# Local attention and a top-2 mixture of experts in one kernel: the routing steps are handed out by their VectorE time, and the array's products come a turn after what they read

## The chip, the cores and the metric

The kernel runs on one core of a Trainium2 chip. The metric is the device time of one execution, in microseconds (us). A core has five engines that run their own instruction streams in program order: TensorE (PE in the profile, "the array"), VectorE (DVE), ScalarE (ACT), GpSimd (POOL) and SyncE (SP, which here only issues DMAs). They wait for each other by semaphores.

## The reference

Attention within chunks of 64 tokens gives 4608 rows of 512 numbers; a noisy gate then sends each row to the two best of 8 experts, and the two results are added by their weights:

```python
scores = scale * np.matmul(q_c, k_c.transpose(0, 1, 2, 4, 3))   # 8 x 8 x 576 x 64, chunks of 64
attn = softmax(scores)
x = np.matmul(attn, v_c)  ->  x: (4608, 512)
logits = x @ w_gate
noise_scale = np.log1p(np.exp(x @ w_noise))
noisy_logits = logits + noise_scale * noise
top2 = np.argpartition(-noisy_logits, 2, axis=1)[:, :2]          # weights: softmax over the two
for e in range(8):
    for k in range(2):
        mask = top2[:, k] == e
        h = np.maximum(x[mask] @ w1[e], 0.0)                     # w1: 8 x 512 x 1024
        out[mask] += top2_w[mask, k, None] * (h @ w2[e])         # w2: 8 x 1024 x 512
```

## The kernel before, in words

**Three stages.** The 4608 tokens are 36 tiles of 128. `attend(it)` (L677) is one turn of the attention stage: it holds the scores of tile `it` (L410), the product with v of tile `it-2` (L437), the transposes of the probabilities of tile `it-1` (L426) and of the finished rows of tile `it-3` (L457). Every fourth turn adds the gate's products (L464), and the turn after that their sum over four parts (L476). VectorE has four instructions in each turn: the maximum `mx` (L414), the subtraction `pr` (L419), the reciprocal `rc` (L445) and the division `xs` (L449). ScalarE has the exponential (L422) and three copies out of PSUM (L442, L428, L458). SyncE loads q, k and v four turns ahead and stores the finished rows to a DRAM buffer `xbuf`. Turns 36 to 40 finish the last tiles, and four of them lie inside the first expert block.

After that come the expert blocks, 24 of them, three per expert. Block i gathers its rows of `xbuf` by a list, transposes them (`x_tile`, L288, then `xh` L295 on ScalarE and `xl` L296 on VectorE), multiplies by w1 (`layer1`, 8 steps f of 12 matmuls, L305) and by w2 (`layer2`, per 128 rows 8 steps f of 3 matmuls, also L305). All products are made of three, from a high and a low part. So each layer 1 step needs `hh` (L323, ScalarE) and `hl` (L324, VectorE) after it, each layer 2 tile `o` (L343, VectorE), and a store (L272, an indirect DMA that GpSimd issues). During layer 1 of block 0 the w2 of expert 0 is split into its parts (`w2h` L137, `w2l` L138).

**Routing.** The lists are made by `route(g)` (L481) for five groups of tiles: 8, 8, 4, 8 and 8. It is a Python generator; each `yield` ends a step, and its instructions go into the streams where the caller asks for the next step. Per group there are: four ScalarE instructions (L494 to L497), the noisy logits (L501 to L509), the two best of eight (L514, L518), their one-hot form (L523 to L529), a rank by nine small products on the array (L535, L537), positions and weights (L540 to L582; for the last group also an order of the experts, L556 to L572). Then each tile of the group is built: `gohp` half on GpSimd (L598) and half on ScalarE (L599, L600), `geq` on VectorE (L602), `grhs` on GpSimd, in the last group on VectorE (L606); and two products place it into one PSUM bank (L590, four matmul records). Last, the bank is added to `acc` (L624), and after groups 1, 3 and 4 the list of block 0, 1 or 2 is written (`finish_lists`, L207 to L211) and its rows are gathered (L240, indirect DMAs on GpSimd).

**What sets the order.** Nothing is scheduled by the compiler: program order is the order of the calls. Before the change `step_route(n)` takes n steps, whatever they cost: 10 in a turn (15 from turn 35), 2 after each quarter of a layer 1 step and 2 after each layer 2 step of blocks 0 and 1. Only the oldest group moves. `IDLE` puts 7 empty steps where another engine's answer is awaited, and a tile's products follow its `grhs` by some steps:

```python
            yield
            yield
            built.append((r, ohp, rhs))
            if len(built) > 2:
                yield
                place(*built.pop(0))
            yield
```

Of the kernel before, what the change touches and what calls it, by code (L numbers as in the profile page):

```python
# [8 lines left out]
FT = mybir.dt.float32  # L9
# [51 lines left out]
def kernel(ctx, tc, qT, kT, vh, wgn, noise, w1, w2, out, caps=CAPS):  # L61
# [417 lines left out]
    IDLE = 7  # L479

    def route(g):  # L481
# [16 lines left out]
        for _ in range(IDLE):  # L498
            yield

        V.scalar_tensor_tensor(u, u, -1.0, y, op0=OP.add, op1=OP.subtract)  # L501
        yield
        V.tensor_sub(sp, sp, u)
        yield
        V.scalar_tensor_tensor(sp, z[:, :, 1, :], 0.0, sp, op0=OP.max, op1=OP.add)
        yield
        V.tensor_mul(sp, sp, nz[:, t0:t0 + G, :])
        yield
        V.tensor_add(sp, sp, z[:, :, 0, :])  # L509
        yield  # L510
        m = gate.tile(n8, FT, name="gm")
        mi = gate.tile(n8, U32, name="gmi")
        for r in range(G):
            V.max(m[:, r], sp[:, r])  # L514
            if r % 2:
                yield
        for r in range(G):
            V.max_index(mi[:, r], m[:, r], sp[:, r])  # L518
            if r % 2:
                yield  # L520
        oh = gate.tile([P, 2, G, NE], FT, name="goh")
        for k in range(2):
            V.tensor_tensor(oh[:, k], be(e_row), br(mi[:, :, k]), OP.is_equal)  # L523
            yield
# [5 lines left out]
        yield  # L530
        nc.scalar.activation(ex, ex, AF.Exp)
        for _ in range(IDLE + 4 if g == LAST else IDLE):
            yield
        rk = PS[:, 7, 256:256 + 8 * (G + 1)].rearrange("p (g e) -> p g e", e=NE)
# [3 lines left out]
        for _ in range(IDLE):  # L538
            yield
# [4 lines left out]
        yield  # L544
# [3 lines left out]
        yield  # L548
# [3 lines left out]
        yield  # L552
        if g == LAST:
# [10 lines left out]
            yield  # L564
# [8 lines left out]
            yield  # L573
# [3 lines left out]
        yield  # L577
        pj = gate.tile([P, 2, 2, G], I32, name="gpj")
        pf = gate.tile([P, 2, 2, G], FT, name="gpf")
# [3 lines left out]
        yield  # L583

        lp = PS[:, 7, 0:2 * NL]
        built = []

        def place(r, ohp, rhs):
            for k in range(2):
                nc.tensor.matmul(lp, ohp[:, k], rhs[:, k].rearrange("p c n -> p (c n)"),  # L590
                                 start=(r == 0 and k == 0), stop=(r == G - 1 and k == 1))
# [3 lines left out]
        for r in range(G):  # L595
            t = t0 + r
            ohp = gate.tile([P, 2, P], FT, name="gohp", bufs=3)
# [6 lines left out]
            yield  # L604
            rhs = gate.tile([P, 2, 2, NL], FT, name="grhs", bufs=3)
            B.tensor_tensor(rhs, eq[:, :, None, :].to_broadcast([P, 2, 2, NL]),  # L606
                            vals[:, :, t, :, None].to_broadcast([P, 2, 2, NL]), OP.mult)
            yield
            yield
            built.append((r, ohp, rhs))  # L610
            if len(built) > 2:
                yield
                place(*built.pop(0))
            yield
        while built:
            for _ in range(3):
                yield
            place(*built.pop(0))
        yield
# [11 lines left out]
        if g == LAST:  # L631
            for c in range(2):
                for js in (slice(0, NJ // 2), slice(NJ // 2, NJ)):
                    n = [P, js.stop - js.start, NE, NE]
                    by = gate.tile([P, 2, 2, NL], FT, name="grhs", bufs=3).rearrange("p a b n -> p (a b n)")
# [4 lines left out]
                    yield  # L640
# [15 lines left out]
    def finish_route(until=lambda: not routing):  # L656
        while not until():
            step_route(1)
# [18 lines left out]
    def attend(it):  # L677
        STEPS = 2 if it < 35 else 3
# [15 lines left out]
        if it - 5 >= 0 and (it - 5) % 4 == 3:  # L694
            gate_sum((it - 5) // 4)
            if grp_of[it - 5] != grp_of.get(it - 4):
                routing.append(route(grp_of[it - 5]))
# [41 lines left out]
    def hook_tail(f, d):  # L739
# [6 lines left out]
        else:  # L746
            step_route(2)

    for i in range(NBL + 1):
# [27 lines left out]
        def hook2_r(k, f):  # L777
            hook2_f(k, f)
            step_route(2)
# [11 lines left out]
        if i < NBL:  # L791
            layer1(i, hook1, hook_tail if i == 0 else lambda f, d: step_route(2))
# [160 lines left out]
```

## Time and profile before

| | |
|---|---|
| median of 3 runs | 1007.67 us (1004.89 to 1007.74) |
| the profiled execution's own time | 996.2 us |
| its span in the trace | 994.4 us |
| PE, DVE, ACT, POOL busy | 96%, 46%, 31%, 49% of the span |
| VectorE's first `mx` of the attention stage, and its last | 5.4 us and 132.1 us |
| the first expert matmul (L305) | 139.2 us |

The profile gives times in us from the start of the span. A row of the timeline has start, duration, engine, line, operation, out<-in and count; what stands in brackets is how long the engine had been idle before it, and who ended that. A row of the groups has the busy time of the group in us and the mean of one instruction in ns. The share "PEclk" is the array's granted clock, 1.00 being full speed. Busy shares are averages over stages with different limits, so each stage is read by itself.

### The profile page before, as it was taken

To read this page: it belongs to the slowest core of one execution; us is meant where nothing else is said; L and a number is where in the kernel's file an instruction comes from. 1 tells how busy PE (TensorE), PEld (TensorE's weight loads), DVE (VectorE), ACT (ScalarE), POOL (GpSimd) and SP (SyncE) were. 2 spreads that over 40 slices of the span, in tenths; PEclk is the share of its full clock that TensorE was granted. 3 is DMA by queue.
4 is the path that set the end of the run, shared out by engine and by line. 5 is a ranking of instruction groups with operands and counts; after the bars stand their busy time and mean duration, and the time that the engine had idled before them with its cause. 6 is when DMAs were issued, how large, how long until landed. Compare 5 with 4: busy or idle time off the path is not lost.

```text
span 994.4 us, 18553 instructions
## 1 busy us (share of the span) xinstructions
PE 955.1 (96%) x7353; PEld 855.4 (86%) x7353; DVE 459.3 (46%) x1001; ACT 307.9 (31%) x689; POOL 485.4 (49%) x619
## 2 busy tenths in 40 slices
PE   6898989999999999999999999999999999999994
PEld 5677769888799998998899899989998999899984
DVE  6678876543445442534253434343444344434311
ACT  4667764312232221322131223122322231223100
POOL 1043534426677776177617772677167616601111
PEclk9989999999999999999999999999999999999998
DMA  9998968332513452245214522552245223511212
GB/s 336 377 340 271 323 228 310 63 102 54 146 46 81 111 151 50 44 122 150 51 33 128 148 51 36 135 140 58 68 96 140 58 70 94 136 20 22 32 25 41
DMA packets 60362, 121.54 MB, mean 122 GB/s; under 512 B 9280, under 2 KB 10176, under 8 KB 60272
## 3 DMA queue, kind: packets, MB, share of 16 engines
q1 hardware_dynamic: 40112, 81.64, 23.2%
q0 software_dynamic: 20160, 38.69, 20.8%
q8 instruction: 58, 0.95, 0.4%
q14 instruction: 32, 0.26, 0.1%
HBM read 81.56 MB, written 38.73 MB: 121 GB/s over the span
## 4 chain that ended last, share of the span: by engine, by line
PE 84%; DVE 2%; ACT 1%; issue 0%; POOL 0%; DVEq 0%; ACTq 0%; POOLq 0%
PE PS L305 80%; PE PS L590 1%; PE PS L334 1%; PE PS L288 0%; DVE xl L296 0%; ACT xh L295 0%; PE PS L464 0%; DVE o L343 0%; POOL grhs L606 0%; DVE xs L449 0%; PE PS L222 0%; ACT xt L458 0%; PE PS L437 0%; ACT gohp L599 0%; DVE gmi L518 0%
## 5 line engine op out<-in xcount | busy, mean ns | idle before, releaser
L260 POOL DMA_INDIRECT xg<-xbuf,piece x257 | 265.9, 1035 | 72.6 <-issue 66.3
L305 PE MATMUL PS<-xh,w1h 128*128 128x384 f32 (+2 forms) x768 | 262.9, 342 | 1.9 <-ACT xh L295 1.1
L305 PE MATMUL PS<-xl,w1h 128*128 128x384 f32 (+2 forms) x768 | 260.5, 339 | 0.3 <-DVE xl L296 0.3
L305 PE MATMUL PS<-xh,w1l 128*128 128x384 f32 (+2 forms) x768 | 260.6, 339 | 0.0
L272 POOL DMA_INDIRECT out<-o,lid x73 | 116.9, 1601 | 246.5 <-DVE o L343 234.4
L305 PE MATMUL PS<-w2h,hh 128*128 128x512 f32 x584 | 229.5, 393 | 0.0
L305 PE MATMUL PS<-w2h,hl 128*128 128x512 f32 x584 | 228.4, 391 | 0.0
L305 PE MATMUL PS<-w2l,hh 128*128 128x512 f32 x584 | 228.3, 391 | 0.0
L323 ACT ACTIVATE hh<-PS 128x384 fp32r<-128x384 f32 (+1 forms) x192 | 93.9, 490 | 362.3 <-PE PS L305 362.3
L324 DVE SCALAR_TENSOR_TENSOR hl<-PS,hh 128x384 fp32r<-128x384 f32 (+1 forms) x192 | 107.0, 558 | 181.1 <-ACT hh L323 181.1
L343 DVE TENSOR_SCALAR o<-PS,lwt 128x512 f32<-128x512 f32 x73 | 54.7, 749 | 235.4 <-PE PS L305 235.4
L305 PEld LDWEIGHTS PS<-xh,w1h 128*128 128x128 f32 x768 | 144.3, 188 | 5.4 <-ACT xh L295 1.5
L305 PEld LDWEIGHTS PS<-xl,w1h 128*128 128x128 f32 x768 | 144.3, 188 | 2.3 <-DVE xl L296 0.5
L305 PEld LDWEIGHTS PS<-xh,w1l 128*128 128x128 f32 x768 | 144.2, 188 | 0.9
L305 PEld LDWEIGHTS PS<-w2h,hl 128*128 128x128 f32 x584 | 109.5, 188 | 23.6
L305 PEld LDWEIGHTS PS<-w2h,hh 128*128 128x128 f32 x584 | 109.7, 188 | 23.2 <-issue 0.8
L305 PEld LDWEIGHTS PS<-w2l,hh 128*128 128x128 f32 x584 | 109.7, 188 | 22.4
L295 ACT ACTIVATE xh<-y 128x512 fp32r<-128x512 f32 x67 | 41.2, 615 | 104.8 <-DVE y L292 104.8
L598 POOL TENSOR_SCALAR gohp<-row_p,gpf 128x128 f32<-128x128 f32 x36 | 25.1, 707 | 95.8 <-DVE gpf L582 71.6
L296 DVE TENSOR_TENSOR xl<-y,xh 128x512 fp32r<-128x512 f32 x67 | 45.0, 672 | 48.0 <-ACT xh L295 48.0
L292 DVE STREAM_TRANSPOSE y<-xg 128x512 f32<-128x512 f32 x67 | 45.6, 680 | 3.2 <-DMA xg<-xbuf,piece 3.2
L138 DVE TENSOR_TENSOR w2l<-st,w2h 128x512 fp32r<-128x512 f32 x64 | 44.4, 693 | 0.0
(139 smaller groups left out, 783.7 us busy)
## 6 DMA issues: line engine op xcount, KB each, us to landing
st<-in_w SPq DMA_DIRECT2D x56, 512.0 KB, 5.0
out<-zero SPq DMA_DIRECT2D x37, 256.0 KB, 4.0
vb<-in_vh SPq DMA_DIRECT2D x36, 260.0 KB, 4.9
qp<-in_qT SPq DMA_DIRECT2D x36, 256.0 KB, 4.5
kb<-in_kT SPq DMA_DIRECT2D x36, 256.0 KB, 5.3
xbuf<-xs SPq DMA_DIRECT2D x36, 256.0 KB, 4.4
xg<-xbuf,piece POOLq DMA_INDIRECT x257, 2.7
st<-in_w SPq DMA_DIRECT2D x16, 256.0 KB, 5.7
```

The lines of the kernel that those rows point to most:

```text
L138: (eng or nc.vector).tensor_sub(lo[:, s], st[:, s], hi[:, s].bitcast(FT))
L260: nc.gpsimd.indirect_dma_start(out=XG[e, j][:, t * P:(t + 1) * P], out_offset=None, in_=xpieces, in_offset=bass.IndirectOffsetOnAxis(ap=pi ...
L272: s = nc.gpsimd.indirect_dma_start(out=to, out_offset=bass.IndirectOffsetOnAxis(ap=rows, axis=0), in_=o, in_offset=None, compute_op=OP.add)
L292: nc.vector.transpose(y[:, 0:4 * r], x[:, 0:4 * r])
L295: nc.scalar.activation(oh, src, AF.Copy)
L296: nc.vector.tensor_sub(ol, src, oh.bitcast(FT))
L305: nc.tensor.matmul(p, a, b, start=first and n == 0, stop=last and n == 2)
L323: nc.scalar.activation(hh[:, 0:m], p, AF.Relu)
L324: nc.vector.scalar_tensor_tensor(hl[:, 0:m], p, 0.0, hh[:, 0:m].bitcast(FT), op0=OP.max, op1=OP.subtract)
L334: nc.tensor.matmul(p[32 * q:32 * q + 32, 0:P], HF[0][:, f, 32 * t:32 * t + 32], w[:, q * P:(q + 1) * P], start=(f == 0), stop=(f == NF - 1))
L343: nc.vector.tensor_scalar(o[0:r], p[0:r], weights_of(i, j)[0:r], None, op0=OP.mult)
L598: nc.gpsimd.tensor_scalar(ohp[:, 0], row_p, pf[:, 0, 0, r:r + 1], None, op0=OP.is_equal)
```

## The change

Routing steps now yield what they cost on VectorE in us (0.15 to 0.8). `step_route(us, n)` moves a counter `clock` on by n and hands out steps until their sum has used up `us`: 1.3 us and n = 6 in an attention turn, 0.6 and 0.5 after each quarter of a layer 1 step in blocks 0 and 1, 1.0 and n = 2 after each layer 2 step. A `yield None` makes the group wait until the counter has moved on by `TURN` = 6, `yield "next"` until it has moved at all. When the oldest group waits, the next one is given steps, up to the point where it would need the shared PSUM bank. A tile costs `TILE` = 0.6, so up to three tiles are built in a turn (before: two), and a tile's products are placed when it is `TURN` old or when more than two are built. `gohp` and `grhs` get four buffers (before: three), `gpj` and `gpf` two. The rank goes to bank 6 while an older group holds bank 7.

```diff
-    IDLE = 7
+    TURN, TILE = 6, 0.6
+    clock, turn, flushing = [0], [0], []
...
         nc.scalar.activation(sp, u, AF.Ln)
-        for _ in range(IDLE):
-            yield
+        yield None
...
         V.scalar_tensor_tensor(u, u, -1.0, y, op0=OP.add, op1=OP.subtract)
-        yield
+        yield 0.22
...
         nc.scalar.activation(ex, ex, AF.Exp)
-        for _ in range(IDLE + 4 if g == LAST else IDLE):
-            yield
-        rk = PS[:, 7, 256:256 + 8 * (G + 1)].rearrange("p (g e) -> p g e", e=NE)
+        yield None
+        while routing[0][0] != g and (turn[0] % 4 == 2 or turn[0] in (NT - 4, NT - 3) or turn[0] > NT):
+            yield "next"
+        at = 7 if routing[0][0] == g else 6
+        rk = PS[:, at, 256:256 + 8 * (G + 1)].rearrange("p (g e) -> p g e", e=NE)
         nc.tensor.matmul(rk, before, ohb, start=True, stop=False)
...
+        while routing[0][0] != g:
+            yield "next"
...
         for r in range(G):
+            while built and (clock[0] - built[0][3] >= TURN or len(built) > 2):
+                place(*built.pop(0))
             t = t0 + r
-            ohp = gate.tile([P, 2, P], FT, name="gohp", bufs=3)
+            ohp = gate.tile([P, 2, P], FT, name="gohp", bufs=4)
...
-            built.append((r, ohp, rhs))
-            if len(built) > 2:
-                yield
-                place(*built.pop(0))
-            yield
+            built.append((r, ohp, rhs, clock[0]))
+            yield TILE
         while built:
-            for _ in range(3):
-                yield
+            while clock[0] - built[0][3] < TURN and not flushing:
+                yield "next"
             place(*built.pop(0))
...
-    def step_route(n):
-        for _ in range(n):
-            while routing:
+    def step_route(us, n=1):
+        clock[0] += n
+        for item in list(routing):
+            while us > 0:
+                if clock[0] < item[2] and not flushing:
+                    break
                 try:
-                    next(routing[0])
+                    cost = next(item[1])
+                except StopIteration:
+                    routing.remove(item)
                     break
-                except StopIteration:
-                    routing.pop(0)
+                if isinstance(cost, float):
+                    us -= cost
+                else:
+                    item[2] = clock[0] + (1 if cost else TURN)
+            if us <= 0:
+                return
...
-            step_route(5 * STEPS)
+            step_route(1.3, TURN)
...
-            step_route(2)
+            step_route(0.6)
...
-            step_route(2)
+            step_route(1.0, 2)
...
-            layer1(i, hook1, hook_tail if i == 0 else lambda f, d: step_route(2))
+            layer1(i, hook1, hook_tail if i == 0 else lambda f, d: step_route(0.5))
```

The order of the instructions moves at many places; three of them matter below. The lines of `route` lie 1 to 5 higher in the new file (L590, the placing, is L593 there; L598 is L603; L602 and L606 are L607 and L610).

The first place is VectorE in turns 12 and 13, where group 0 starts: four instructions of attention make a turn, and `gu` is the first routing step that reads what ScalarE made. Before:

```order
L414 TENSOR_REDUCE mx<-PS 128x8
L419 TENSOR_TENSOR pr<-PS,mx 128x2x4x64
L445 RECIPROCAL rc<-rc 128x8
L449 TENSOR_TENSOR xs<-PS,rc 128x2x4x64
L501 SCALAR_TENSOR_TENSOR gu<-gu,gy 128x64
L503 TENSOR_TENSOR gsp<-gsp,gu 128x64
L505 SCALAR_TENSOR_TENSOR gsp<-gz_655,gsp 128x64
```

After:

```order
L449 TENSOR_TENSOR xs<-PS,rc 128x2x4x64
L414 TENSOR_REDUCE mx<-PS 128x8
L419 TENSOR_TENSOR pr<-PS,mx 128x2x4x64
L445 RECIPROCAL rc<-rc 128x8
L449 TENSOR_TENSOR xs<-PS,rc 128x2x4x64
L501 SCALAR_TENSOR_TENSOR gu<-gu,gy 128x64
L503 TENSOR_TENSOR gsp<-gsp,gu 128x64
L505 SCALAR_TENSOR_TENSOR gsp<-gz_655,gsp 128x64
L507 TENSOR_TENSOR gsp<-gsp,nz 128x64
```

The first `xs` of the second piece is that of turn 12: `gu` has moved behind the four instructions of turn 13.

The second place is the array in layer 2 of block 0, second tile of rows (steps f = 0 and 1 of it, then f = 2). `w2h`, `w2l` are the parts of w2, `hh`, `hl` those of the hidden rows. Before:

```order
L305 MATMUL PS<-w2h_2984,hh_2825 128x512
L305 MATMUL PS<-w2l_2985,hh_2825 128x512
L305 MATMUL PS<-w2h_2984,hl_2826 128x512
L305 MATMUL PS<-w2h_2984,hh_2827 128x512
L305 MATMUL PS<-w2l_2985,hh_2827 128x512
L305 MATMUL PS<-w2h_2984,hl_2828 128x512
L305 MATMUL PS<-w2h_3069,hh_2829 128x512
```

After:

```order
L305 MATMUL PS<-w2h_2962,hh_2834 128x512
L305 MATMUL PS<-w2l_2963,hh_2834 128x512
L305 MATMUL PS<-w2h_2962,hl_2835 128x512
L305 MATMUL PS<-w2h_2962,hh_2836 128x512
L305 MATMUL PS<-w2l_2963,hh_2836 128x512
L305 MATMUL PS<-w2h_2962,hl_2837 128x512
L593 MATMUL PS<-grhs,gohp 128x160 x2
L305 MATMUL PS<-w2h_3045,hh_2838 128x512
```

The first placing of the last group (L593) now stands after 30 of the 72 layer 2 matmuls of block 0; before, it stood in layer 1 of block 1, after all 72 and 9 more. The rank of that group (L537, L539) now stands after 9 of them, before after 42.

The third place is GpSimd in the same stage, from the gather of block 1's rows (`xg<-xbuf`) on: `out<-o` are the stores of block 0. Before:

```order
L240 DMA xg<-xbuf,lid_124 128x512 x3
L271 MEMSET spacer 1x1
L272 DMA out<-o,lid_123 4736x512
L271 MEMSET spacer 1x1
L272 DMA out<-o,lid_123 4736x512
L598 TENSOR_SCALAR gohp<-row_p,gpf 128x128 x2
L271 MEMSET spacer 1x1
L272 DMA out<-o,lid_123 4736x512
L598 TENSOR_SCALAR gohp<-row_p,gpf 128x128 x6
```

After:

```order
L240 DMA xg<-xbuf,lid_124 128x512 x3
L271 MEMSET spacer 1x1
L272 DMA out<-o,lid_123 4736x512
L603 TENSOR_SCALAR gohp<-row_p,gpf 128x128 x8
L240 DMA xg<-xbuf,lid_125 128x512 x3
```

All eight `gohp` of the last group have moved between the first and the second store. On VectorE the same stage now has, in this order: the rest of the rank's one-hots, the last `hl` and `w2l`, positions and order of the experts, `xl` of block 1's first tile, `o` of block 0's first tile, and then the eight pairs of `geq` and `grhs`; before, three `o`, the third `xl` and two `hl` stood among those.

More of the change, by code (lines that the diff above doesn't have):

```diff
@@ L497, in route @@
         nc.scalar.activation(sp, u, AF.Ln)
-        for _ in range(IDLE):
-            yield
+        yield None
         V.scalar_tensor_tensor(u, u, -1.0, y, op0=OP.add, op1=OP.subtract)
-        yield
+        yield 0.22
         V.tensor_sub(sp, sp, u)
-        yield
+        yield 0.22
         V.scalar_tensor_tensor(sp, z[:, :, 1, :], 0.0, sp, op0=OP.max, op1=OP.add)
-        yield
+        yield 0.22
         V.tensor_mul(sp, sp, nz[:, t0:t0 + G, :])
-        yield
+        yield 0.22
         V.tensor_add(sp, sp, z[:, :, 0, :])
-        yield
+        yield 0.22
         m = gate.tile(n8, FT, name="gm")
@@ L515, in route @@
             if r % 2:
-                yield
+                yield 0.16
         for r in range(G):
@@ L519, in route @@
             if r % 2:
-                yield
+                yield 0.15
         oh = gate.tile([P, 2, G, NE], FT, name="goh")
@@ L537, in route @@
             nc.tensor.matmul(rk[:, k:G + 1], ones, ohb[:, 0:G + 1 - k], start=False, stop=(k == G))
-        for _ in range(IDLE):
-            yield
+        yield None
         V.tensor_scalar(sm, ex, 1.0, 1e-9, op0=OP.add, op1=OP.add)
@@ L547, in route @@
         V.reciprocal(wt[:, 0], sm)
-        yield
+        yield 0.4
         ohr = gate.tile([P, 2, G, NE], FT, name="gohr")
@@ L576, in route @@
         V.tensor_mul(wt[:, 1], ex, wt[:, 0])
-        yield
-        pj = gate.tile([P, 2, 2, G], I32, name="gpj")
-        pf = gate.tile([P, 2, 2, G], FT, name="gpf")
+        yield 0.45
+        pj = gate.tile([P, 2, 2, G], I32, name="gpj", bufs=2)
+        pf = gate.tile([P, 2, 2, G], FT, name="gpf", bufs=2)
         V.tensor_scalar(pj[:, 0], lii[:, :, ts], NE * (P - 1), None, op0=OP.bitwise_and)
@@ L603, in route @@
                             pf[:, 1, :, r:r + 1].to_broadcast(n2), OP.is_equal)
-            yield
-            rhs = gate.tile([P, 2, 2, NL], FT, name="grhs", bufs=3)
+            rhs = gate.tile([P, 2, 2, NL], FT, name="grhs", bufs=4)
             B.tensor_tensor(rhs, eq[:, :, None, :].to_broadcast([P, 2, 2, NL]),
                             vals[:, :, t, :, None].to_broadcast([P, 2, 2, NL]), OP.mult)
-            yield
-            yield
-            built.append((r, ohp, rhs))
-            if len(built) > 2:
-                yield
-                place(*built.pop(0))
-            yield
+            built.append((r, ohp, rhs, clock[0]))
+            yield TILE
         while built:
-            for _ in range(3):
-                yield
+            while clock[0] - built[0][3] < TURN and not flushing:
+                yield "next"
             place(*built.pop(0))
-        yield
+        yield "next"
         av = acc.rearrange("p c n -> p (c n)")
@@ L634, in route @@
                     n = [P, js.stop - js.start, NE, NE]
-                    by = gate.tile([P, 2, 2, NL], FT, name="grhs", bufs=3).rearrange("p a b n -> p (a b n)")
+                    by = gate.tile([P, 2, 2, NL], FT, name="grhs", bufs=4).rearrange("p a b n -> p (a b n)")
                     by = by[:, 0:n[1] * NE * NE].rearrange("p (j r e) -> p j r e", r=NE, e=NE)
@@ L677, in attend @@
     def attend(it):
-        STEPS = 2 if it < 35 else 3
+        turn[0] = it
         if it < NT:
@@ L696, in attend @@
             if grp_of[it - 5] != grp_of.get(it - 4):
-                routing.append(route(grp_of[it - 5]))
+                routing.append([grp_of[it - 5], route(grp_of[it - 5]), 0])
         if it - 4 >= 0 and (it - 4) % 4 == 3:
```

23 lines of the change are left out of this document (12 added, 11 removed).

## The prediction

> **What bounds the kernel now.** The chain of waits is first: the array's instructions are most of it. Next I read busy time by stretches (start:end in us; length; busy time and count of PE, PEld, DVE, ACT, POOL; clock; DMA share; GB/s).
>
> ```profile
> 41.00:112.74 71.74, 62.70 (x1512) 52.72 (x1502) 57.61 (x183) 54.04 (x139) 31.73 (x40) 0.95 0.92 315
> 49.96:56.79 6.83, 6.19 (x100) 5.27 (x91) 6.43 (x38) 3.15 (x7) 0.00 (x0) 0.50 0.98 340
> 165.45:166.78 1.33, 1.33 (x9) 1.24 (x8) 1.18 (x7) 0.69 (x3) 0.00 (x0) 1.00 1.03 380
> 179.84:183.64 3.80, 3.80 (x21) 3.17 (x19) 3.35 (x21) 0.00 (x0) 1.59 (x1) 1.00 0.36 39
> 236.00:990.00 754.00, 745.95 (x4014) 676.68 (x4012) 303.03 (x502) 183.57 (x386) 403.49 (x505) 1.00 0.35 83
> ```
>
> The array ends the chain, and from 236 us on it is busy for 745.95 of 754.00 us. The change touches nothing there, so whatever time the array loses or wins before 236 us moves the end by as much. Two stretches count: the attention stage, and blocks 0 and 1. In the first of them the waits between 41 and 63 us (who waits, for whom; total, times, longest) show what sets the turns:
>
> ```profile
> PE PS L410 <- DVE pr L419: 2.5, 2, 1.8
> DVE gu L501 <- ACT gsp L497: 2.3, 1, 2.3
> ...
> DVE gr L546 <- PE PS L537: 1.6, 1, 1.6
> ```
>
> VectorE stands for 2.3 us because its routing step `gu` follows in the same turn the four ScalarE instructions that it reads. Then the array waits up to 1.8 us for VectorE's `pr`, and in the stretch from 49.96 us, right after it, its clock is 0.50 for 6.83 us. In blocks 0 and 1 (136 to 236 us) these are all the array's waits but one of 1.1 us:
>
> ```profile
> PE PS L305 <- ACT xh L295: 1.1, 1, 1.1
> PE PS L305 <- DVE hl L324: 0.8, 1, 0.8
> PE PS L535 <- DVE gohb L527: 0.6, 1, 0.6
> PE PS L305 <- DVE xl L296: 0.3, 1, 0.3
> ```
>
> So in the blocks there are under 4 us to win, and since the array has no slack there, every placing or rank that comes before its operands costs in full. That is why each of them is timed below: when the array is there, by its matmuls, and when VectorE and GpSimd are, by the instructions ahead.
>
> **Attention: what the turns gain.** With `gu` a turn later its 2.3 us of wait lie beside the next turn's work; the same goes for `gr`, 1.6 us: 3.9 us in all, and the clock's fall goes with the first. Against it stands GpSimd, which now has up to three tiles in a turn (groups of L598, L606 and of the w1 parts, 62 to 110 us; busy, mean ns, idle):
>
> ```profile
> L606 POOL TENSOR_TENSOR grhs<-geq,vals 128x320 f32<-128x320 f32 x16 | 11.6, 723 | 0.8 <-DVE geq L602 0.8
> L598 POOL TENSOR_SCALAR gohp<-row_p,gpf 128x128 f32<-128x128 f32 x16 | 10.7, 669 | 65.6 <-DVE gpf L582 58.9 <-PE PS L437 6.8
> L138 POOL TENSOR_TENSOR w1l<-st,w1h 128x512 fp32r<-128x512 f32 x8 | 10.3, 1282 | 9.2 <-ACT w1h L137 9.2
> ```
>
> Three tiles are 3 × (0.669 + 0.723) = 4.18 us, with a `w1l` 5.46 us, more than the 4.25 us between two `mx` at 112.81 and 117.06 us. Such turns give back some; I take a gain of 3.4 us until turn 31 (ends 1.4 and 5.3: GpSimd giving back 2.5 of the 3.9, or nothing, with 1.4 more from the clock).
>
> **Attention: what the gather takes back.** The list of block 0 and the first gather behind it, and the array's first transposes of those rows:
>
> ```profile
> 112.74 0.17 DVE L211 CAST lid<-lfl 128x3 int32<-128x3 f32 x1
> 112.81 0.69 DVE L414 TENSOR_REDUCE mx<-PS 128x8 f32<-128x512 f32 x1
> ...
> 117.06 0.67 DVE L414 TENSOR_REDUCE mx<-PS 128x8 f32<-128x512 f32 x1
> ```
>
> ```profile
> L240 POOL DMA_INDIRECT xg<-xbuf,lid x1: 1203/1203/1203, 113.2 to 113.2; - x1
> ...
> DMA to landing us min/median/max: 6.6/6.6/6.6
> ```
>
> ```profile
> 124.03 0.60 PE L288 MATMUL PS<-ident,xg 128*128 128x128 f32 x4
> ```
>
> Before, the rows are there at 113.2 + 6.6 = 119.8 us, 4.2 us ahead of the array. After, group 1's bank is added up at the end of turn 31 rather than 29, two turns later. With the 3.4 us that is 112.74 + 2 × 3.8 − 3.4 = 116.9 us (3.8 us is my estimate of these turns, between the 4.25 above and the shorter ones that follow), and the rows land at about 123.8 us. The array comes at 124.03 − 3.4 = 120.6 us, with some 1.3 us of other work that it has before the first transposes; it waits about 1.9 us. Whatever the turns gain moves both alike. Attention's net is −3.4 + 1.9 = **−1.5 us** (ends +0.5 and −3.4).
>
> **Layer 1 of block 0.** The wait for `hl` at 147.17 us follows a placing group that moves away: **−0.8**. Group 3's placings now start after 48 of the 96 matmuls, at the end of step f = 3. From there on, the array's pace (the chain of waits in order of time: start, length, instructions):
>
> ```profile
> 163.24 1.04 PE PS L305 x6
> 164.29 0.54 PE PS L590 x4
> ...
> 171.63 4.81 PE PS L305 x21
> ```
>
> A w1 matmul is 0.173 us, a placing of four records 0.54, a w2 matmul 0.229. A placing every three matmuls comes each 3 × 0.173 + 0.54 = 1.06 us, while GpSimd makes a tile in 1.39 us by the groups above, about 1.3 where the two overlap. The first placing waits behind this chain of step f = 2, whose anchor in before is:
>
> ```profile
> 150.56 0.96 PE L476 MATMUL PS<-sel,ls 128*128 128x16 f32 x8
> ```
>
> ```profile
> 153.32 0.65 DVE L602 TENSOR_TENSOR geq<-row_je,gpf 128x160 f32<-128x160 f32 x2
> ```
>
> The first `geq` came 2.76 us after the sums began; with GpSimd's `grhs`, 0.72, a placing could go at about 3.9 us (0.4 for the semaphores and the `geq` itself), and the array, with 12 matmuls and 0.8 us of sums, is there at 2.9. So it waits 1.0, and then 4 × (1.3 − 1.06), some 0.9, until `gohp` and `grhs` have caught up: **+1.9 us** (ends 0, if both are made while the array still has its step to do, and 4.0).
>
> **The last group's rank** now stands after 9 w2 matmuls. From group 3's last placing the array needs 18 × 0.173 + 9 × 0.229 = 5.2 us. VectorE needs the sum into `acc` and the list (1.33 us, the stretch from 165.45), the steps L501 to L529, and between them the last `hl` and `w2l`:
>
> ```profile
> 168.08 0.22 DVE L501 SCALAR_TENSOR_TENSOR gu<-gu,gy 128x64 f32<-128x64 f32 x1
> ...
> 172.30 0.69 DVE L296 TENSOR_TENSOR xl<-PS,xh 128x512 fp32r<-128x512 f32 x1 [0.94 <-ACT xh L295]
> 172.91 0.21 DVE L523 TENSOR_TENSOR goh<-row,gmi 128x64 f32<-128x64 f32 x1
> ...
> 173.39 0.74 DVE L343 TENSOR_SCALAR o<-PS,lwt 128x512 f32<-128x512 f32 x1
> ```
>
> ```profile
> L324 DVE SCALAR_TENSOR_TENSOR hl<-PS,hh 128x384 fp32r<-128x384 f32 x16 | 8.7, 555 | 13.5 <-ACT hh L323 13.5
> L138 DVE TENSOR_TENSOR w2l<-st,w2h 128x512 fp32r<-128x512 f32 x8 | 5.5, 693 | 0.0
> ```
>
> The steps are (172.30 − 0.94 − 168.08) + (173.39 − 172.91) = 3.76 us. Instructions overlap by some 0.05 to 0.08 us, so `hl` and `w2l` count 0.5 and 0.6. In all 1.33 + 0.1 + 3.76 + 0.5 + 0.6 = 6.3, and the array waits **+1.1 us**.
>
> **The last group's first placing** stands after 30 w2 matmuls. Without waits the array is there at 5.2 + 0.2 (nine small products, an estimate) + 21 × 0.229 = 10.2 us, and with the wait for the rank and the transposes of block 1's first tile (0.6, as in the row of L288) at 11.9. VectorE goes on from 6.3: the last `hl` and `w2l` (with ScalarE's `hh` ahead, which stands behind the exponential that L529 releases) to 8.5; L540 to L582 in 3.80 us (the stretch from 179.84); between them `xl` 0.6 and `o` 0.7: 13.6 us. Then GpSimd:
>
> ```profile
> 174.41 1.65 POOL L272 DMA_INDIRECT out<-o,lid  x1 [3.69 <-DVE o L343]
> 175.47 0.62 POOL L271 MEMSET spacer<- 1x1 f32 x1
> ```
>
> The store of block 0's first tile stands ahead of the eight `gohp`, and GpSimd is free 175.47 − 174.41 = 1.06 us after `o`; the first `gohp` takes 0.67 and its semaphore, 0.8: 15.4 to 15.5 us. The array waits **+3.7 us** (ends 0 and 4.5). Behind it wait the two later tiles of layer 2, and nobody else's work fills the array. The next placings come each 3 × 0.229 + 0.54 = 1.2 us, against 0.67 for GpSimd's part of a tile, so they don't wait.
>
> **The clock.** A wait of 1.8 us was followed by two stretches of 3.4 us at 0.50 in before. In the wait of 3.7 us a stretch of that length is mostly idle, and the array, which is then never idle, does 3.4 us of its work at half speed: 1.7 us lost: **+1.7** (ends 0 and 3.4, two such stretches). [...]
>
> **Start of block 1's layer 1.** The list of block 2 has moved ahead of the third `xl`; the waits for `xh` and `xl` (1.1 + 0.3) become about 1.9: **+0.5** (ends 0 and 1.5). The rest costs nothing: SP's order does not change, no matmul is added, four buffers for three take no time, and the `w1l` of GpSimd move by some tiles in stretches where the array does not wait for them.
>
> **Sum:** −1.5 − 0.8 + 1.9 + 1.1 + 3.7 + 1.7 + 0.5 = +6.6 us. The profiled execution would go from 996.2 to 1002.8 us; it lies 11.5 us under the median, whose runs reach from 1004.89 to 1007.74 us, so I add the sum to the median: 1007.67 + 6.6 = 1014.3 us.
>
> **Rivals.** 0.3%, about what a measurement of this kernel can tell, is 3.0 us.
>
> [...]
>
> *The last group does not hold the array* (0.22): if VectorE's steps overlap more, or ScalarE's `hh` come earlier, so that its `gpf` is done before 10.2 us instead of 13.6, the waits of 1.1 and 3.7 and the clock's 1.7 go: +6.6 − 6.5 = +0.1, 1007.8 us. Against it stands that the lengths are measured and the order is fixed.
>
> *VectorE alone sets the attention turns* (0.16), the faster side. Between 41 and 112.74 us it is busy for 57.61 of 71.74 us (the first stretch) and idles 14.1; if that all goes, because no turn has to wait for what another engine made in it, attention's net is −14.1 + 1.9 = −12.2 instead of −1.5, and the sum is 6.6 − 10.7 = −4.1: 1003.6 us. It decides from a gain of 13 us on (6.5 if the last group does not hold the array). GpSimd's 5.46 us in a turn speak against it.
>
> *A later gather and a second fall of the clock* (0.08): the list 1.9 us later, since GpSimd's tiles lengthen, and another 3.4 us at half speed in layer 1: 6.6 + 1.9 + 1.7 = +10.2, 1017.9 us.
>
> That the change doesn't do what it says is excluded by the order of the instructions, printed above.
>
> **The numbers.** The forecast has 0.40; slower is 0.40 + 0.14 + 0.08 = 0.62, same 0.22, faster 0.16. The range reaches from 1003.5, at the faster case, to 1017.5, just under the last rival; the likeliest case's own range, with attention's and the clock's ends, is 1010.5 to 1017.5.
>
> **What would show it.** Right: `gu` without idle time before it; the array waiting for `xg` at the first transposes of block 0; waits of L593 for `grhs` in layer 1 of block 0 and for `gohp` or `grhs` after 30 w2 matmuls of its layer 2, near 3.7 us, with a stretch at 0.50 behind. Wrong: the first expert matmul over 5 us earlier than 139.2, or no wait at that placing.

## The result, and the profile after

The changed kernel takes 1015.23 us (median of 5 runs, 1014.32 to 1017.39) where the kernel before takes 1004.89 (5 runs, 1003.11 to 1007.74): +10.3 us, ratio 1.010, 95% interval 1.0075 to 1.0125. It is slower, as forecast; the forecast sum was +6.6 us.

The chips differ. Beside eight of the ten experiments below the kernel before takes 996 us, beside the other two 1002.6. The first trace of the kernel before is of 996.2 us, the first trace of the change of 1015.23 us, so the two cannot be subtracted. The changed kernel was therefore traced a second time, where the kernel before takes 996.16 us (experiment after_again, 1006.41 us), and rows below are from that second trace unless the text says otherwise. Two executions took far longer than all others, one of late_last (1916.66 us) and one of the kernel before beside after_again (1591.54 us): the medians count them, the ratios do not.

One piece of the difference between the first two traces can be named. It is the group of products L334 in block 3's stage, of the change and then of the kernel before (busy, mean ns, idle before and its releaser):

```profile
L334 PE MATMUL PS<-st,hf 128*32 128x128 f32 x128 | 7.2, 347 | 2.4 <-issue 2.4
```

```profile
L334 PE MATMUL PS<-st,hf 128*32 128x128 f32 x128 | 3.7, 273 | 0.0
```

The array waits 2.4 us in it for nothing that the profile shows, and its clock is 0.50 from 327.15 to 330.57 us. The second trace of the change has 3.7 us and no wait there, as the kernel before; so the change alone does not make it.

Now the chain of waits of the first trace of the change, by engine:

```profile
PE 79%; issue 2%; DVE 2%; SPq 1%; POOL 1%; DMA 0%; ACT 0%; POOLq 0%; ACTq 0%; DVEq 0%
```

The array still ends it. The array's waits in blocks 0 and 1 (136 to 260 us of the second trace; total, times, longest) answer to the four rows of before:

```profile
PE PS L593 <- POOL gohp L603: 3.8, 1, 3.8
PE PS L305 <- DVE xl L296: 1.8, 1, 1.8
PE PS L537 <- DVE gohb L527: 1.2, 2, 0.9
PE PS L593 <- POOL grhs L610: 1.1, 3, 0.8
PE PS L222 <- DVE xv L218: 1.1, 1, 1.1
```

The wait for `hl` is gone, and 3.85 us for the last group's first `gohp` have come. In the stretches of the second trace behind such waits (the clock is the third number from the end of a row), six have a clock under full speed:

```profile
178.40:181.80 3.40, 1.46 (x5) 1.46 (x6) 2.19 (x6) 0.95 (x4) 3.40 (x5) 0.76 0.61 78
181.80:185.20 3.40, 3.40 (x16) 2.98 (x16) 1.85 (x5) 1.82 (x6) 2.22 (x4) 0.73 0.27 98
198.80:202.20 3.40, 2.93 (x13) 2.93 (x14) 1.08 (x2) 0.15 (x1) 2.88 (x4) 0.78 0.76 169
202.20:205.60 3.40, 3.40 (x16) 3.40 (x15) 0.56 (x1) 0.80 (x2) 0.00 (x0) 0.72 0.79 165
229.40:232.80 3.40, 3.40 (x21) 3.06 (x21) 0.65 (x2) 0.00 (x0) 0.70 (x1) 0.79 0.00 0
232.80:236.20 3.40, 3.40 (x14) 2.63 (x14) 0.96 (x2) 0.60 (x1) 2.00 (x3) 0.71 0.06 19
```

Each pair is one spell of half speed of about 3.4 us: (0.24 + 0.27) × 3.4 = 1.73 us lost, (0.22 + 0.28) × 3.4 = 1.70, (0.21 + 0.29) × 3.4 = 1.70. They lie behind the waits of 3.85, 1.83 and 1.14 us. The kernel before has one, behind its 1.14 us wait for `xv`:

```profile
219.00:222.40 3.40, 3.35 (x19) 3.15 (x20) 0.65 (x2) 0.00 (x0) 0.00 (x0) 0.74 0.00 0
222.40:225.80 3.40, 3.40 (x15) 2.75 (x14) 0.75 (x1) 0.59 (x1) 1.91 (x3) 0.76 0.06 19
```

In the attention stage of the second trace the clock is whole from 41 to 61.26 us, where before had 6.83 us at half:

```profile
41.00:61.26 20.26, 17.28 (x486) 14.45 (x475) 16.80 (x65) 13.87 (x34) 0.00 (x0) 1.00 1.02 371
```

The account of the two stages, before and the change's second trace: the first expert matmul at 139.2 and 139.1 us; from there to block 2's first matmul 91.2 and 101.5 us; the span 994.4 and 1004.8. Between these two traces all 10.3 us lie in blocks 0 and 1. They are made of waits of the array, 3.9 and 9.4 us; of L305, 72.0 and 74.9; of the placings, 7.0 and 8.9 (for each matmul the time until the next one starts, without waits).

The first trace of the change divides its time otherwise: its first expert matmul is at 145.5 us, and from there to block 2 it takes 98.4 us, 7.2 more than before. Its blocks have the same waits (9.4 us) and placings (9.0), but L305 takes 71.8 us, since one spell of half clock lies in them and not three. What its attention stage lost can't be told, since no trace of the kernel before was taken beside it.

### The profile page after: what moved, and what is told of

Its sections match the earlier page's. It is cut to its first block, busy times and chain, and to the rows that moved or that the text cites. A ratio compares the mean times of both kernels' runs of the same rounds, so it can differ in the third digit from the quotient of the medians.

```text
span 1013.3 us, 18557 instructions
## 1 busy us (share of the span) xinstructions
PE 961.6 (95%) x7353; PEld 857.8 (85%) x7353; DVE 462.8 (46%) x1001; ACT 309.6 (31%) x689; POOL 479.6 (47%) x619
## 4 chain that ended last, share of the span: by engine, by line
PE 79%; issue 2%; DVE 2%; SPq 1%; POOL 1%; DMA 0%; ACT 0%; POOLq 0%; ACTq 0%; DVEq 0%
PE PS L305 77%; PE PS L334 1%; SPq L678 1%; PE PS L593 1%; POOL gohp L603 0%; DMA out<-zero 0%; PE PS L288 0%; POOL grhs L610 0%; DVE xl L296 0%; DVE gaccp L638 0%; DVE grhs L636 0%; POOL xg L240 0%; DVE o L343 0%; DVE xs L449 0%; PE PS L222 0%
## 5 line engine op out<-in xcount | busy, mean ns | idle before, releaser
L260 POOL DMA_INDIRECT xg<-xbuf,piece x257 | 260.3, 1013 | 78.7 <-issue 63.3
L305 PE MATMUL PS<-xl,w1h 128*128 128x384 f32 (+2 forms) x768 | 260.4, 339 | 1.8 <-DVE xl L296 1.8
L305 PE MATMUL PS<-xh,w1h 128*128 128x384 f32 (+2 forms) x768 | 261.8, 341 | 0.0
L305 PE MATMUL PS<-xh,w1l 128*128 128x384 f32 (+2 forms) x768 | 260.4, 339 | 0.0
L305 PE MATMUL PS<-w2h,hh 128*128 128x512 f32 x584 | 229.5, 393 | 0.0
L305 PE MATMUL PS<-w2h,hl 128*128 128x512 f32 x584 | 228.1, 391 | 0.0
L305 PE MATMUL PS<-w2l,hh 128*128 128x512 f32 x584 | 228.0, 390 | 0.0
L305 PEld LDWEIGHTS PS<-xl,w1h 128*128 128x128 f32 x768 | 144.2, 188 | 3.9 <-DVE xl L296 2.1
L305 PEld LDWEIGHTS PS<-xh,w1h 128*128 128x128 f32 x768 | 144.3, 188 | 3.1 <-issue 0.8
L305 PEld LDWEIGHTS PS<-xh,w1l 128*128 128x128 f32 x768 | 144.2, 188 | 0.9
L343 DVE TENSOR_SCALAR o<-PS,lwt 128x512 f32<-128x512 f32 x73 | 54.5, 749 | 192.0 <-PE PS L305 142.0
L305 PEld LDWEIGHTS PS<-w2h,hl 128*128 128x128 f32 x584 | 109.4, 187 | 23.5
L305 PEld LDWEIGHTS PS<-w2h,hh 128*128 128x128 f32 x584 | 109.4, 187 | 23.0 <-issue 0.8
L305 PEld LDWEIGHTS PS<-w2l,hh 128*128 128x128 f32 x584 | 109.4, 187 | 22.2
L603 POOL TENSOR_SCALAR gohp<-row_p,gpf 128x128 f32<-128x128 f32 x36 | 26.6, 820 | 93.0 <-DVE gpf L583 92.0
```

The lines of the kernel that those rows point to most:

```text
L260: nc.gpsimd.indirect_dma_start(out=XG[e, j][:, t * P:(t + 1) * P], out_offset=None, in_=xpieces, in_offset=bass.IndirectOffsetOnAxis(ap=pi ...
L305: nc.tensor.matmul(p, a, b, start=first and n == 0, stop=last and n == 2)
L343: nc.vector.tensor_scalar(o[0:r], p[0:r], weights_of(i, j)[0:r], None, op0=OP.mult)
L603: nc.gpsimd.tensor_scalar(ohp[:, 0], row_p, pf[:, 0, 0, r:r + 1], None, op0=OP.is_equal)
```

## The experiments

Theory behind the first four: the change loses in both stages, by its turns of three tiles and late groups in the first, and in the second since the array meets the last group's rank and placings before their operands. Rivals: chance between executions, and that the next late thing takes over when one wait is moved.

**before_again.** No edit.

> The kernel before, unchanged, for a second profiled execution. The two traces differ by 13.5 us at the start of block 2 and by 19.4 us from block 4 on; the extra 5.9 us lie in one run of the array's L334 products (9.8 us instead of 3.9, with gaps in which the array waits for no engine). Theory: those 5.9 us are not the change's; they come and go from one execution to the next, and the first profile of before (994.4 us) was a lucky one. Then this one has such gaps somewhere behind 236 us and a span of 1000 to 1006 us, with the first expert matmul at 139 us and block 2's start near 230 us again. Rival: the gaps are the change's own; then the span is 994 to 997 us again.

Measured: 996.54 us, span 994.7; first expert matmul 139.7, block 2 at 230.9 us, no gap in L334. The rival's number, though not its reason: after_again shows that the gap is not the change's either. It goes with the chip in all twelve traces: the nine from chips where the kernel before takes 996 us have no gap there, the three others have one.

**old_attention.** The counters are those of before until the expert blocks begin (a step per yield, 7 for `yield None`, 10 steps in a turn, the oldest group alone), and a tile's products are placed as before:

```diff
+        if old:
+            for _ in range(10 if turn[0] < 35 else 15):
+                if debt[0]:
+                    debt[0] -= 1
+                    continue
...
     attend(NT)
+    old.clear()
```

> The changed kernel, with the steps of the attention turns (up to turn 36) handed out as before: the array's order up to the first expert matmul is that of before, and from there on that of the change. Theory: the change loses in both stages, 6.3 us up to the first expert matmul and 7.2 us from there to block 2. Then the first expert matmul is at 139 us (138.5 to 140.5) instead of 145.5, the stretch from there to block 2 still takes 98 us, and the time is 5 to 7 us under the changed kernel's: 1009 to 1011 us. Rival: the attention stage is limited by what does not change (DMA, the clock, chance), and the first expert matmul stays at 143 us or later: 1013 to 1016 us.

Measured: 1007.92 us, ratio 1.0109 (1.0092 to 1.0126). Its trace has the first expert matmul at 143.4 us in the very order of the kernel before, and the blocks take 101.6 us. A miss, and for the first expert matmul the rival's number: the attention stage of before, alone, saves nothing against the 1.0102 of after_again. The blocks are as in after_again, three spells included. The time at the 19th maximum was 70.9 us here and 66.6 and 67.1 in the two traces of before, with one order: the first turns vary by some 4 us.

**late_last.**

```diff
         n2 = [P, 2, NL]
+        if g == LAST:
+            yield None
+            yield None
```

> The changed kernel, where the last group waits two TURNs more between its positions and its first tile, so that its first placing stands after 48 of the layer 2 matmuls of block 0 instead of 30. Theory: the wait of 3.85 us at that placing and the half clock behind it (1.7 us) go, since 18 matmuls (4.1 us) have moved in front of it: 5 us less, 1009 to 1011 us, and no wait over 1 us there. Rival: what is late next takes the place of it (the stores, now ahead of the tiles on GpSimd, or the placings that move towards block 1): a wait of 2 us or more elsewhere before block 2, and 1013 to 1016 us.

Measured: 1005.16 us, ratio 1.0091 (1.0068 to 1.0115). The array's longest waits in blocks 0 and 1 of its trace:

```profile
PE PS L305 <- DVE xl L296: 2.7, 1, 2.7
PE PS L593 <- DVE geq L610: 2.2, 1, 2.2
```

The placing's wait fell from 3.85 to 2.2 us, and the one for `xl` rose from 1.8 to 2.7: the first expert matmul to block 2 takes 97.7 us. The rival holds in the main. On VectorE the second `xl`, for which it stands 2.07 us until ScalarE's `xh` is there, and the second `o` now stand between the `geq` of that group, so moving the steps of one group later doesn't free the array. One spell of half clock lies in these blocks, and none behind the 2.7 us.

**fast_chain.**

```diff
-            yield TILE
+            yield 1.0 if turn[0] < NT else TILE
...
-            step_route(1.3, TURN)
+            step_route(2.0, TURN)
```

> The changed kernel with 2.0 us of steps in an attention turn instead of 1.3, and a tile that costs 1.0 there instead of 0.6, so that a group is ready for its tiles a turn or two earlier and two tiles are built in a turn instead of three. Theory: in the attention stage the change loses by turns of three tiles (5.1 us each, GpSimd busy throughout) and by late groups; with two a turn these turns take 4.5 us or less and the first expert matmul comes at 141 to 143 us: 1011 to 1013 us. Rival: the time of these turns is set by all the work in them, VectorE's too, and two tiles beside more of VectorE's steps win nothing: first expert matmul at 145 us or later, 1014 to 1017 us.

Measured: 1009.01 us, ratio 1.0118 (1.01 to 1.0136). From the 19th maximum to the last it takes 67.3 us, against 70.8 in after_again and 65.5 before; the first expert matmul is at 141.7 us. So the turns are shorter, as the theory says, although the clock is halved from 90.5 to 100.8 us, but the time isn't: the blocks take 103.9 us, with 1.9 us of wait for group 3's `grhs`, 1.5 for block 1's rows and 3.8 at the last group's placing.

**after_again.** No edit.

> The changed kernel, unchanged, beside the same runs of the kernel before as the other three. The first trace of it came from runs in which the kernel before took 1004.9 us, the trace of the kernel before from one of 996.2 us, so differences between those two traces may hold some that the change did not make (the 5.9 us in L334, gaps for no engine and 3.4 us of half clock around 125 and 137 us). Theory: the change's own part is some 3 to 4 us up to the first expert matmul and 6 to 8 us from there to block 2; the first expert matmul at 142 to 143 us, block 2's start at 239 to 242 us, no gap in L334: 9 to 12 us over the kernel before in the same runs. Rival: the whole 13.5 us are the change's, first expert matmul at 145 us and block 2 at 243 to 244.

Measured: 1006.41 us, ratio 1.0102 (1.0087 to 1.0117), +10.25 us: the theory's time. The stages are split otherwise than it says: the first expert matmul at 139.1 us and block 2 at 240.6, so nothing is lost in attention here and 10.3 us in the blocks. The time agrees because the two misses cancel.

**old_blocks.** The edit of old_attention, turned around: the old counting begins where the expert blocks begin. One detail is not as before: the last group waits 7 steps after its exponential, where before had 11.

```diff
+            for _ in range(15 if n == TURN else 2):
...
     attend(NT)
+    old.append(1)
```

> The changed kernel, with the steps in the expert blocks handed out as before (two steps after each quarter or step, 15 in a turn that lies in block 0); the attention turns up to 36 keep the change's order. Theory: from the first expert matmul to block 2 it takes 91 us as before instead of 98, with no wait over 1.2 us there, and the time is 6 to 8 us under the changed kernel's and 2 to 5 us over the kernel's before. Rival: the work that the attention stage now leaves to the blocks lengthens them in any order; then 95 us or more, and less than 3 us under the changed kernel's.

Measured: 999.47 us beside 996.16, ratio 1.0039 (1.0025 to 1.0052). The blocks take 91.0 us, 6.9 us under the changed kernel in time. The first expert matmul is at 142.0 us, with one spell of half clock behind a wait for a placing at 130.6. The array's longest waits in the blocks:

```profile
PE PS L305 <- DVE hl L324: 2.4, 2, 1.6
PE PS L222 <- DVE xv L218: 1.1, 1, 1.1
```

One wait is over the 1.2 us that were expected (`hl`, 1.6). The rest is as the theory says: the order within blocks 0 and 1 makes the larger part of the loss, and it can be had back with the attention stage of the change.

**before_idle.** The kernel before with one number changed.

```diff
-        for _ in range(IDLE):
+        for _ in range(IDLE + 4 if g == 0 else IDLE):
             yield
```

> The kernel before, where only the first group waits 11 empty steps instead of 7 after its four ScalarE instructions, so that VectorE's first step of it stands a turn later, as the change does it. Theory: VectorE's wait of 2.3 us goes and with it the array's wait of 1.8 and the half clock from 50 to 57 us; the 19th maximum comes at 63 to 65 us instead of 66.6, and if nothing takes it back, the time is 2 to 4 us under the kernel's before. Rival: what is won by turn 18 is given back until the last maximum, since the loads of q, k and v or the group's later work set the pace: within 1 us of the kernel before.

Measured: 994.66 us beside 996.16, ratio 0.9983 (0.9972 to 0.9994). It is the one version whose interval lies under the kernel before, by 1.5 us. The stretch that was at half clock in before:

```profile
49.96:56.79 6.83, 5.42 (x97) 3.23 (x100) 5.74 (x29) 2.23 (x7) 0.00 (x0) 0.75 1.03 371
```

VectorE no longer waits for ScalarE's logarithm, and one spell is gone of two. The 19th maximum is at 65.0 us. Between theory (2 to 4 us) and rival (under 1).

**fast_old.** fast_chain's two edits in old_blocks.

> The changed kernel with both: 2.0 us of steps in an attention turn and two tiles in it (a tile costs 1.0 there), and the steps in the blocks handed out as before. Theory: the change's losses lie in its turns of three tiles and in the order of the blocks, so with both gone it is within 2 us of the kernel before, or under it by up to 2 if the gain of the first turns stays. Rival: the late lists and the full turn for each answer of another engine cost in any case: 3 us or more over the kernel before.

Measured: 994.83 us beside 996.16, ratio 0.9994 (0.9981 to 1.0008): no difference that can be told. The theory's number: with the turns of three tiles and the new order of the blocks both gone, the loss is gone. In its stretch from the 19th maximum to the last the clock is halved from 88.5 to 95.3 us and again from 129.5; in that of after_again it is never halved.

**fast_three.**

```diff
-                yield 1.0 if turn[0] < NT else TILE
+                yield 0.9 if turn[0] < NT else TILE
```

> As fast_old (2.0 us of steps in an attention turn, blocks as before), but a tile costs 0.9 in an attention turn, so that three are built in it again. It tells apart what makes the stretch from the 19th maximum to the last longer with the change (70.8 to 71.4 us instead of 65.5; fast_old has 67.6). Theory: the turns of three tiles; then the stretch is 69.5 us or more again, with turns of 5.0 us or more where tiles are built. Rival: the late groups; they come early here, so the stretch is 66 to 68 us as in fast_old. The time is 996 to 999 us by the theory and 993 to 996 by the rival, if no wait over 2 us arises in the blocks, where the placings of the last group now come partly in layer 2 of block 0.

Measured: 1010.86 us beside 1002.64, ratio 1.0075 (1.0047 to 1.0102). The stretch from the 19th maximum to the last takes 76.5 us. The array's longest waits from 64 to 160 us:

```profile
PE PS L410 <- DVE pr L419: 4.5, 3, 3.1
PE PS L594 <- POOL grhs L613: 4.4, 4, 3.2
```

The stretch is on the theory's side and beyond it. Part of that is not the tiles' number: the array waits 3.1 us at once for `pr`, and two spells of half clock lie in the stretch (87.5 to 90.9 and 121.6 to 125.0 us). So 76.5 doesn't price the third tile. The time doesn't either, since the wait of 3.2 us for `grhs` lies in block 0, where the expectation had allowed none over 2 us.

**mid_old.** As fast_old, with 1.65 and 0.85 for 2.0 and 1.0.

> As fast_old, but 1.65 us of steps in an attention turn and a tile at 0.85: still two tiles in a turn, and fewer of VectorE's steps in the turns where fast_old's array waits 2.1 and 1.9 us for VectorE's subtraction. Theory: those two waits shrink below 1.3 us each, as with the change's 1.3 us a turn, the halved clock behind them goes, and the stretch from the 19th maximum to the last takes 65 to 67 us: 1 to 3 us under the kernel before. Rival: the steps only move to other turns, and the stretch stays at 67 to 68 us: within 1 us of fast_old.

Measured: 1001.81 us beside 1002.64, ratio 0.9992 (0.9975 to 1.0008). Neither: the waits for `pr` are 1.2, 1.8 and 1.4 us in its trace and the stretch takes 69.8 us, longer than fast_old's. That the steps only moved to other turns is likely and not shown: this trace and fast_three's come from the chip where the array also waits for nothing that the profile shows (0.8, 0.7 and 0.4 us between 113 and 123 us here), so their stretches don't compare cleanly with the others.

## Why the prediction was right or wrong, point by point

**Right: that it is slower, where in the blocks, and by which waits.** The chain that was worked out for the last group's first placing can be read off the second trace. GpSimd:

```profile
177.61 1.64 POOL L272 DMA_INDIRECT out<-o,lid  x1 [7.68 <-DVE geq L607]
178.72 4.21 POOL L603 TENSOR_SCALAR gohp<-row_p,gpf 128x128 f32<-128x128 f32 x5
```

VectorE:

```profile
176.59 0.74 DVE L343 TENSOR_SCALAR o<-PS,lwt 128x512 f32<-128x512 f32 x1
```

And the array:

```profile
176.09 0.40 PE L305 MATMUL PS<-w2h,hl 128*128 128x512 f32 x1
180.34 0.90 PE L593 MATMUL PS<-grhs,gohp 128*128 128x160 f32 x2 [3.85 <-POOL gohp L603]
```

`o`, then the store that holds GpSimd for 178.72 − 177.61 = 1.1 us, then `gohp`, then the placing, 3.85 us late where 3.7 was forecast. (The store's row names `geq`, which VectorE made meanwhile; the store begins 0.28 us after the end of `o`, as it did before: 174.41 after 173.39 + 0.74.) That the wait came out so near is in part luck: `o` ended some 0.6 us earlier than forecast (12.9 us after group 3's last placing, not 13.6), and the record of the first `gohp` is 1.57 us long where 0.8 was taken, its semaphore included.

`gu` has no idle time before it, as forecast. The rank waits 0.86 (forecast 1.1). The start of block 1's layer 1 waits 1.83 us where before waited 1.35: +0.48 (forecast +0.5). The wait for `hl` of 0.83 us went.

Group 3's placings wait 1.3 us in all, 0.81 at the first and 0.10 to 0.16 at each of the next four, where 1.9 was forecast. They cost more than these waits: the five come 1.43 to 1.50 us apart (153.18, 154.67, 156.14, 157.64, 159.07), and the later ones that wait for nothing 1.07 (161.81 to 162.88), the 1.06 that was taken. The difference that is not wait arises around each wait: the matmul ahead counts to its end, 0.33 us, and not to the start of the next, 0.17, and the first record of the placing takes 0.24 us until the next one and not 0.13. With that, 0.27 us at each of five placings, they cost 2.7 us.

**Right in kind, mis-sized: the clock.** +1.7 us for one spell behind the 3.85 us. In the second trace there are three in the blocks instead of one, so +3.4: the 1.83 us wait brought one as well, which the sum left out though in before's trace a wait of 1.8 us was followed by 6.83 us at 0.50. In the first trace the same waits of 3.85, 1.83 and 1.15 us stand in the blocks, and only the first is followed by a spell: +0 against before.

What differs between the two traces is where the wait lies. Within each trace the spells begin whole multiples of 3.413 us apart (in the second at 180.19, 200.67 and 231.39 us: 6 and 9 times), so the traces can be cut into such windows. The 1.83 us wait lay within one window in the second trace (197.44 to 199.27 us) and across two in the first (203.88 to 205.71 us). These are the windows that hold it or most of it, of the second trace and then of the first (the first busy time is the array's):

```profile
197.26:200.67 3.41, 1.58 (x9) 1.40 (x9) 2.48 (x8) 0.00 (x0) 2.93 (x5) 1.00 0.67 168
```

```profile
204.27:207.69 3.42, 1.98 (x11) 1.98 (x12) 1.98 (x5) 0.00 (x0) 2.93 (x5) 1.00 0.71 176
```

The array was busy for 46% of the first, and a spell followed; for 58% of the other, and none did. Over all twelve traces, from 20 to 980 us, each of the 22 windows at full clock in which the array was busy for less than 48% was followed by a spell; of the 27 between 48% and 60%, four were, and of the windows above 60%, ten. The wait of 1.14 us for `xv`, by itself a third of a window, is followed by a spell in seven of the twelve traces, those in which it begins up to 0.98 us into its window; in the five others, in which it begins 1.15 us in or later, it is not. Why a window that is busy for 67% brings one there stays open. So the clock's term can't be forecast from the waits' lengths alone.

**Not in the sum: the placings' own time.** They take 8.9 us instead of 7.0; part of it is inside the spells. Against before_idle, where L305 and the placings take 70.4 + 6.9 us and no spell lies in the blocks, the second trace has 6.5 us more, of which three spells make 5.1. The other 1.4 us are, to 0.1 us, those around the waits of the placings: 0.27 us at each of group 3's five, as above, and the same matmul counted to its end ahead of the 3.85 us.

**Wrong: attention, −1.5 us, and with it the step "what the gather takes back".** The net is near zero, but of larger parts. The 19th and the last of the 36 maxima, of the second trace and of before:

```profile
61.26 0.68 DVE L414 TENSOR_REDUCE mx<-PS 128x8 f32<-128x512 f32 x1
...
132.07 0.68 DVE L414 TENSOR_REDUCE mx<-PS 128x8 f32<-128x512 f32 x1
```

```profile
66.58 0.69 DVE L414 TENSOR_REDUCE mx<-PS 128x8 f32<-128x512 f32 x1 [1.14 <-PE PS L410]
...
132.13 0.69 DVE L414 TENSOR_REDUCE mx<-PS 128x8 f32<-128x512 f32 x1
```

By the 19th maximum 5.3 us are won, more than the 3.4 taken and as much as the upper end that was given. They were not kept: nearly all of them (5.26 us) are given back by the last maximum. Not the gather does it. The list came later than forecast, at 119.5 us instead of 116.9, but its rows landed 4.9 us after the issue at 119.95 instead of 6.6, and the array's first transposes waited half a microsecond:

```profile
119.48 0.17 DVE L211 CAST lid<-lfl 128x3 int32<-128x3 f32 x1
```

```profile
124.86 0.66 PE L288 MATMUL PS<-ident,xg 128*128 128x128 f32 x4 [0.49 <-DMA xg<-xbuf,lid]
```

What takes it back are, by the rows, the turns of three tiles. The maxima around group 0's tiles, and GpSimd from 64 to 78 us:

```profile
68.94 0.68 DVE L414 TENSOR_REDUCE mx<-PS 128x8 f32<-128x512 f32 x1
73.96 0.68 DVE L414 TENSOR_REDUCE mx<-PS 128x8 f32<-128x512 f32 x1
79.21 0.69 DVE L414 TENSOR_REDUCE mx<-PS 128x8 f32<-128x512 f32 x1 [2.95 <-PE PS L410]
```

```profile
L610 POOL TENSOR_TENSOR grhs<-geq,vals 128x320 f32<-128x320 f32 x8 | 5.7, 718 | 0.0
L603 POOL TENSOR_SCALAR gohp<-row_p,gpf 128x128 f32<-128x128 f32 x8 | 5.4, 680 | 60.9 <-DVE gpf L583 60.9
L138 POOL TENSOR_TENSOR w1l<-st,w1h 128x512 fp32r<-128x512 f32 x2 | 2.6, 1310 | 0.0
```

GpSimd never stops, and a turn lasts about as long as its three tiles and a `w1l`: 5.0 and 5.25 us, as the forecast priced them (up to 5.46). VectorE's 2.95 us of idle time there are a wait for the scores L410, which stand on the array behind three placings. Eight tiles keep GpSimd busy as long as before, 13.7 us, but fewer attention turns pass meanwhile: three maxima lie between the first `gohp` and the last `grhs` of group 0 and three of group 1, where before had four and five. The turns left over must be run afterwards. The forecast took 2.5 us of give-back at most.

A part of the 5.3 us was never a gain, but work put off: before begins four of group 0's tiles ahead of the 19th maximum, the second trace none, so the stretch behind it holds 15 `gohp` there and 19 here, and GpSimd is busy in it for 33.9 and 38.6 us. fast_chain and fast_old, with two tiles a turn, bring the stretch from 70.8 down to 67.3 and 67.6 us, spells of half clock included, and hold 15 and 16 `gohp` in it. So the turns of three tiles and the tiles put off can't be told apart by these runs; that the number of tiles in a turn alone does it is argued and not shown, since fast_chain and fast_old also start each group earlier, and fast_three was disturbed by other waits.

**The rivals.** That the last group would not hold the array: excluded by the 3.85 us. That VectorE alone sets the turns: excluded by the first expert matmul, 12 us earlier by that rival and at 139.1 and 145.5 us in the two traces, and spoken against by GpSimd's rows. The rival of a second fall of the clock came true in the blocks of the second trace and not in those of the first; its later gather did not cost. That the clock does not fall (0.14): excluded by the spell behind the 3.85 us in both traces.

**The size.** −1.5 − 0.8 + 1.9 + 1.1 + 3.7 + 1.7 + 0.5 became, by the second trace and in the same order, about 0 − 0.8 + 1.3 + 0.9 + 3.85 + 3.4 + 0.5 = 9.2 us, less 0.2 for group 3's rank, which waits 0.35 instead of 0.55, and plus the 1.4 around the placings' waits: 10.4, against 10.25 measured. The blocks' part of the forecast, +8.1 us, lies between the 7.2 of the first trace and the 10.3 of the second. Three small slips are in the working: by its own numbers the rows of block 0 would land at 124.0 us and not 123.8, the placing would wait 3.6 us and not 3.7, and the ends of attention and clock reach from 1010.7 to 1018.0 us and not from 1010.5 to 1017.5. That the forecast time, 1014.3 us, lies within 1 us of the 1015.23 measured is luck: the sum was 3.7 us too small, and the median that it was added to, 1007.67, was 2.8 us above the 1004.89 of the five runs.

How the attention stage divides among executions stays open: with one order the first expert matmul came at 139.1, 142.0, 142.4 and, in the first trace, 145.5 us, and old_blocks and old_attention lose 3.3 and 11.5 us, more in sum than the whole change.

## What to carry to other kernels

An instruction on a bound engine is rightly placed when its operands are there, and a planner that counts the time of one engine (VectorE here) doesn't see the queue of another: follow the last operand through every queue, the stores included, before a product is moved forward. Of a change that hands out work anew, take its pieces apart: here one piece, the first group's step a turn later, wins 1.5 us alone, while the whole change loses 10. And give a wait of one or two microseconds a range and not a price: the same 1.83 us cost 1.7 us more by the clock in one trace and nothing more in another. Before a difference of that size between two traces is put down to an order of instructions, count the spells in both.

## What the runs showed of the hardware

Up to 980 us of a trace, a spell of half clock lasted 3.41 us or a multiple of that (6.83 us in before's attention stage) and cost a busy array 1.7 us per 3.41. Within a trace the spells began whole multiples of 3.413 us apart. In the twelve traces all 22 such windows at full clock in which the array was busy for less than 48% were followed by one, whatever the length of a single wait: the same wait of 1.83 us brought a spell where it lay within one window and none where it lay across two. GpSimd's `gohp` followed an indirect store after 1.1 us in the change's second trace, though the store's row is 1.64 us long. The products L334 took 3.7 us where the kernel before takes 996 us, and 4.7 to 7.2, with waits for nothing that the profile shows, in the three traces from chips where it takes 1002.6 or 1004.9: in these twelve traces such gaps go with the chip, and a trace is best compared with one from the same chip.
